# Product 3 of the second sequence matrix made jointly, left forms made as the transform's results come, and results kept on chip

## The chip, the cores and the metric

The kernel runs on one core of one Trainium2 chip, in one launch. The metric is the time of that launch on the device in microseconds (us). Its engines work side by side: TensorE (PE) multiplies matrices, VectorE (DVE) and ScalarE (ACT) do elementwise work, SyncE (SP) and GpSimd (POOL) here only issue transfers (DMA) between the device's memory (HBM) and the chip's. Each engine takes its instructions strictly in the order in which they are written and waits on semaphores for the others.

## What is computed

Two branches of the same shape are mixed by a gate per row. S = 2048 rows, D = 512, F = 1792, all in fp32; A_x is the input of both branches (B_x is not used).

```python
x = A_x
g = _sigmoid((x * gate_w).sum(-1, keepdims=True))
a = einsum("bsd,ed->bse", x, dft_hid_re)           # transform along D
b = einsum("bsd,ed->bse", x, dft_hid_im)
y = einsum("ts,bse->bte", dft_seq_re, a) - einsum("ts,bse->bte", dft_seq_im, b)
gate = x @ W_gate;  up = x @ W_up
h = gate * (gate > 0) * up
out = g * y + (1 - g) * (h @ W_down)
```

The two sequence matrices `dft_seq_re` and `dft_seq_im` (2048x2048, called `cr` and `ci` in the kernel, m = 0 and m = 1) make most of the work.

## The kernel before

**Seven products for eight.** Every large product is cut into 2x2 blocks and made by a scheme of seven block products, numbered 1 to 7 (`ORDER`). It needs sums and differences of the blocks of both factors ahead of the product, and sums of the products behind it. So DVE makes forms of the left factor ("lefts": `l..`, `jl..`), forms of the right factor ("rights": `r..`, `jr..`, `hr..`), and the sums behind the products. For the sequence matrices part of the right forms is made early, during other stages, by `right_sums` (tiles `p..`) and stored to an HBM table `tb`; the table `SUMS` says which and when.

**Three matmuls for one.** To keep fp32's accuracy every operand is split in a high part (rounded to fp32r by ACT, names ending in `h`) and a low part (the rest, by DVE, names ending in `l`); a product is then three matmuls (`PARTS`). A piece of a right factor thus takes a load, an ACT cast and a DVE subtraction of 128x1024 before PE can use it. A matmul here is 128x512 columns wide.

**Stages, in PE's order.** `Direct` and `Block` (bank name `c`) make h for pairs of 128 columns of F, with c the number of the pair and q the half of the rows; h and its forms go to `hd` in HBM. `SpectralBlock` (`a`) makes the transform along D and stores the blocks of its result to `ad`. Two more `Block`s, (1,1) and (0,1), follow as `tail`. `Down` (`z`) multiplies h with W_down and writes (1 - g) times it to `out`. Then come the sequence products: `Sequence` (`z`) makes, for the matrix m and the half p of the output rows, those products among 1 to 7 that are not in `JOINT`; `Joint` (`j..`) makes one output form `of` with all seven products once more on smaller blocks. Before, they run as: Sequence(0,0), Joint of form 3 for m=0, Sequence(0,1), Joint of form 1 for both, Joint of form 2 for m=0, Sequence(1,1), Sequence(1,0), and the last Joint of form 2 for m=1. What m=0 leaves goes to `zd` in HBM and is read back for m=1; results are multiplied by g and added onto `out` by accumulating transfers that POOL issues.

**Who sets the order.** The kernel records its steps with a key (their place, in matmuls) and a planner, `Plan`, puts them in an order before anything runs: it goes through the steps with rough durations of its own (`Step.work`, `Queues`, `LANDING`), sorts DVE and ACT by due times, and gives each tile one of 51 equal pieces of on-chip memory (`UNITS`). Its order alone reaches the chip. SP issues loads, POOL stores and accumulating transfers.

**The start.** Eight matmuls on constant data (`warm`) run while the first pieces of x and of the weights arrive. `Direct` needs the split first blocks `xb11h/l` and `wf0h/l`; the weights of pair c arrive as `wr0`, `wr1` and are split to `w0h`, `w0l` and so on.

Of the kernel before, what the change touches and what calls it, by code (L numbers as in the profile page):

```python
# [9 lines left out]
F32R = mybir.dt.float32r  # L10
# [75 lines left out]
class Step:  # L86


    def __init__(self, key, engine, name, a, k):
# [36 lines left out]
class Queues:  # L126
# [3 lines left out]
    LANDING, LATER = 2.1, 1.5  # L130
# [5 lines left out]
    def serve(self, queues, now, to, done):  # L136
        while True:
            act = [q for q in queues.values() if q and q[0][0] <= now + 1e-9]
            until = min([to, *(q[0][0] for q in queues.values() if q and q[0][0] > now + 1e-9)])
            if act:  # L140
                turn = sum(q[0][2] for q in act)
                n = min(q[0][1] for q in act)
                if now + n * turn <= until:
                    now += n * turn
                    for q in act:
                        q[0][1] -= n
                        if q[0][1] < 1e-9:
                            done(q.pop(0)[3], now)
# [9 lines left out]
    def add(self, step, start):  # L158

        def end(s, t):  # L160
            s.end = t + self.LANDING + (self.LATER if "accum_op" in s.k else 0)

        self.now = self.serve(self.queues, self.now, max(start, self.now), end)
        packets = max(1.0, step.work / (0.166 / 16 * (1.6 if "accum_op" in step.k else 1)))
# [4 lines left out]
class Plan:  # L169
# [4 lines left out]
    MATMUL, WAIT, LANDING = 0.22667, 0.035, 2.1  # L174
# [166 lines left out]
def kernel(ctx: ExitStack, tc, xP, xG, wf, wgu, wd, cr, ci, wri, gw, out):  # L341
# [34 lines left out]
    ad = hbm("ad", 2, 2, 2, 2, P, 4, HD)  # L376
# [3 lines left out]
    lb = hbm("lb", 2, 7, 2, P, 4, HD)  # L380
    tb = hbm("tb", 2, 5, 4, 4, P, 2, N)
    wb = hbm("wb", 7, P, 4, 2, P)
# [90 lines left out]
    class Weights:  # L473
# [24 lines left out]
        def parts(self):  # L498
            return [y for x in self.w for y in x] + [self.w3]
# [24 lines left out]
    JOINT = ((0, 1), (0, 2), (0, 3), (1, 1), (1, 2))  # L524

    SUMS = {(0, 5, 0): 160, (0, 3, 1): 150, (0, 1, 1): 330, (1, 2, 0): 465, (0, 1, 0): 535, (1, 5, 2): 637, (0, 5, 1): 680, (1, 1, 1): 715, (0, 2, 1): 790, (0, 3, 0): 955, (1, 1, 0): 995, (1, 2, 1): 1150, (0, 2, 0): 1270, (1, 5, 1): 1564, (1, 5, 3): 1929, (1, 4, 0): 377}
# [175 lines left out]
    class Spectral:  # L702
# [7 lines left out]

        def prep(self, m, key):
# [11 lines left out]
    class SpectralBlock:  # L723
        def __init__(self, sp, q, ih):
            self.sp, self.q, self.ih = sp, q, ih
            self.s, self.y = buf("s"), buf("y")
            self.o = {b: buf("a" + b, (2, 2, HD)) for b in ("12", "21", "22", "11")}
            self.ps = {k: Pair("a") for k in "ABXDG"}
            for m in ORDER:
# [3 lines left out]
                if m in (2, 7, 3, 4):  # L733
                    op(plan.now + 3, self.out, {2: "11", 3: "12", 4: "21", 7: "22"}[m])
# [729 lines left out]
```

## Time and profile before

| what | us |
|---|---|
| median of 3 runs (lowest, highest) | 785.03 (784.77, 787.34) |
| the profiled execution: own time | 786.9 |
| the profiled execution: span of its instructions | 785.0 |
| PE busy | 777.0 |
| DVE busy | 684.4 |
| ACT busy | 466.1 |
| mean rate of the transfers | 355 GB/s, 278.83 MB in all |

The span runs from the first instruction to the last; times inside it count from its start. The views used here are: the page's totals; the chain of waits, which goes back from the last instruction to what released it, step by step; the timeline of one engine (start, duration, engine, line, operation, output<-inputs, shapes, count, and in brackets the idle time ahead with its releaser); the windows, which give the busy time of every engine in a stretch, the clock that TensorE was granted, and the DMA's share and rate; and the list of waits (who waited for whom: total us, times, longest). All engine code is recorded at one helper line, L123, so instructions are told apart by their tiles. Successive matmuls overlap, so the distance between their starts is their cost, not the duration shown.

### The profile page before, as it was taken

The numbers are of one execution on the slowest core, as the hardware profiler recorded it, in microseconds if no ns is written. First come the engines' busy times: TensorE is split into PE (matmuls) and PEld (weight loads), VectorE is DVE, ScalarE is ACT, GpSimd is POOL, SyncE is SP. The second block draws the span as 40 slices with busy tenths as digits, with TensorE's granted clock in tenths as the row PEclk, the third lists the DMA queues.
The fourth block names the chain that finished last, engine by engine and source line by source line (L and its number), as shares of the span: only waits on it lengthen the run. The fifth ranks groups of instructions, "written<-read, shape, count | busy, mean of one in ns | idle before, by whom it ended". The sixth has DMA issues, their size and how long they took to land.

```text
span 785.0 us, 10154 instructions
## 1 busy us (share of the span) xinstructions
PE 777.0 (99%) x3416; PEld 642.2 (82%) x3416; DVE 684.4 (87%) x773; ACT 466.1 (59%) x653; POOL 122.8 (16%) x197
## 2 busy tenths in 40 slices
PE   9899999999999999999999999999999999999997
PEld 7788888888888888888888888888888887888886
DVE  6899999799699652899996699999989999989896
ACT  5545545343446544566675385487588986855762
POOL 0031332323132222211100000110100000002000
PEclk9999999999999999999999999999999999999999
DMA  8975999999998999989999999999999999999964
GB/s 317 391 308 224 358 401 411 416 390 420 401 360 289 355 405 419 418 328 410 415 298 332 411 395 408 295 299 324 349 374 408 411 410 376 341 359 341 326 207 108
DMA packets 80213, 278.83 MB, mean 355 GB/s; under 512 B 9120, under 2 KB 9888, under 8 KB 80160
## 3 DMA queue, kind: packets, MB, share of 16 engines
q1 hardware_dynamic: 53120, 180.52, 60.0%
q0 software_dynamic: 26896, 97.53, 35.6%
q8 instruction: 27, 0.44, 0.2%
q14 instruction: 26, 0.21, 0.1%
q10 hardware_dynamic: 144, 0.13, 0.0%
HBM read 185.86 MB, written 92.28 MB: 354 GB/s over the span
## 4 chain that ended last, share of the span: by engine, by line
PE 86%; DMA 5%; issue 4%; DVE 3%; ACT 0%; SPq 0%; POOL 0%; DVEq 0%; POOLq 0%; ACTq 0%
PE z L123 35%; PE c L123 31%; PE a L123 10%; PE jB L123 3%; PE jA L123 3%; DMA x<-xP 2%; DMA wr<-wgu 2%; PE jX L123 2%; PE jD L123 1%; DMA out<-z 1%; PE jG L123 1%; DVE r L123 1%; DVE cl L123 1%; DVE jcl L123 1%; SPq L123 0%
## 5 line engine op out<-in xcount | busy, mean ns | idle before, releaser
L123 PE MATMUL z<-ch,ll 128*128 128x512 f32 x484 | 188.4, 389 | 0.3 <-ACT z L123 0.3
L123 PE MATMUL z<-cl,lh 128*128 128x512 f32 x484 | 188.5, 389 | 0.2 <-DVE cl L123 0.2
L123 PE MATMUL z<-ch,lh 128*128 128x512 f32 x484 | 188.3, 389 | 0.0
L123 PEld LDWEIGHTS z<-cl,lh 128*128 128x128 f32 x484 | 90.8, 188 | 19.8 <-DVE cl L123 0.8
L123 PEld LDWEIGHTS z<-ch,ll 128*128 128x128 f32 x484 | 90.8, 188 | 19.5 <-ACT z L123 0.7
L123 PEld LDWEIGHTS z<-ch,lh 128*128 128x128 f32 x484 | 90.8, 188 | 18.8
L123 ACT CAST ch<-r 128x1024 fp32r<-128x1024 f32 x72 | 74.1, 1052 | 40.8 <-DVE r L123 33.6
L123 DVE TENSOR_TENSOR cl<-r,ch 128x1024 fp32r<-128x1024 f32 x72 | 86.9, 1221 | 6.8 <-ACT ch L123 5.1
L123 DVE TENSOR_TENSOR p<-p,p 128x1024 f32<-128x1024 f32 x64 | 77.1, 1220 | 10.6 <-DMA p<-ci 8.6
L123 DVE TENSOR_TENSOR jcl<-jr,jch 128x1024 fp32r<-128x1024 f32 x70 | 83.6, 1219 | 2.0 <-ACT jch L123 1.9
L123 ACT ACTIVATE c<-c 128x512 f32<-128x512 f32 x78 | 45.6, 585 | 63.0 <-PE c L123 50.2
L123 ACT CAST jch<-jr 128x1024 fp32r<-128x1024 f32 x70 | 71.0, 1050 | 4.7 <-DVE jr L123 1.6
L123 DVE TENSOR_TENSOR cl<-hr,ch 128x1024 fp32r<-128x1024 f32 (+1 forms) x56 | 59.6, 1088 | 11.4 <-ACT ch L123 5.3
L123 ACT CAST ch<-hr 128x1024 fp32r<-128x1024 f32 (+1 forms) x56 | 52.0, 945 | 25.5 <-PE z L123 14.1
L123 POOL DMA_DIRECT2D tb<-p x64 | 35.0, 546 | 126.2 <-DVE p L123 115.2
L123 PE MATMUL c<-xh,w2l 128*128 128x512 f32 x104 | 40.8, 393 | 2.5 <-ACT c L123 2.5
L123 PE MATMUL c<-xh,w2h 128*128 128x512 f32 x104 | 40.9, 394 | 0.0
L123 PE MATMUL c<-xl,w2h 128*128 128x512 f32 x104 | 40.9, 394 | 0.0
L123 PE MATMUL c<-xh,w1l 128*128 128x512 f32 x104 | 40.5, 389 | 0.0
L123 PE MATMUL c<-xl,w1h 128*128 128x512 f32 x104 | 40.5, 389 | 0.0
L123 PE MATMUL c<-xh,w1h 128*128 128x512 f32 x104 | 40.5, 389 | 0.0
L123 ACT COPY z<-z 128x512 f32<-128x512 f32 x52 | 29.6, 584 | 15.3 <-PE z L123 14.4
(237 smaller groups left out, 1592.3 us busy)
## 6 DMA issues: line engine op xcount, KB each, us to landing
tb<-p POOLq DMA_DIRECT2D x64, 512.0 KB, 9.6
hr<-hd SPq DMA_DIRECT2D x42, 512.0 KB, 7.4
jr<-tb SPq DMA_DIRECT2D x40, 512.0 KB, 10.2
p<-cr SPq DMA_DIRECT2D x32, 512.0 KB, 8.9
p<-ci SPq DMA_DIRECT2D x32, 512.0 KB, 8.2
hd<-hs POOLq DMA_DIRECT2D x28, 512.0 KB, 8.8
r<-tb SPq DMA_DIRECT2D x24, 512.0 KB, 11.0
l<-ad SPq DMA_DIRECT2D x18, 512.0 KB, 9.1
```

The lines of the kernel that those rows point to most:

```text
L123: getattr(getattr(nc, self.engine), self.name)(*map(ap, self.a), **{k: ap(x) for k, x in self.k.items()})
```

## The change

**Joint stages.** All of forms 1, 2 and 3 are now made jointly for both matrices: `Joint((0,1), of)` three times, and `Sequence` keeps products 5, 6, 7, 4 for m=0 and 7, 6, 5, 4 for m=1. The order is J1, S00, S01, J3, S10, S11 and the last J2. By the program, PE has 3,416 matmuls before and after, but 48 instead of 24 of them are 256 columns wide: that is twelve 512-wide matmuls less.

**Left forms.** `SpectralBlock` now makes the forms 5, 7, 6, 3 of the left factor itself, with 16 more DVE subtractions of 128x1024 behind its blocks, and stores all seven forms to `ad` (28 stores in place of 16); the separate passes that loaded the blocks, made the sums and stored them to `lb` are gone (10 stores and their loads). A sign moves from the evacuation into the weights `v` (`minus`).

**Kept on chip.** What Sequence m=0 leaves stays in its tiles for m=1 (`first`), so 6 stores to `zd`, 4 loads and 2 accumulating transfers go. The weights of c=1 are used three blocks in a row, since block (1,1) moves from the tail to the fourth place, and their 7 stores to `wb` and 7 loads go.

**Planner.** Its durations and the keys (`AT`, `SUMS`) are other numbers, so nearly every order changes. `right_sums` makes 72 forms in place of 64.

In all, DVE has 12 more instructions of 1024 columns and 13 more of 512; SP issues one load of 512 KB and two of 256 KB less, POOL seven transfers of 512 KB less, four of them accumulating ones.

```diff
-            self.work = n * 4 * P / 4096 * 0.166 / 16 * (1.6 if "accum_op" in k else 1)
+            self.work = n * 4 * P / 4096 * 0.160 / 16 * (2 if "accum_op" in k else 1)
...
-            self.work = 0.163 + n * 1.0625e-3
+            self.work = 0.156 + n * 1.039e-3
...
-    LANDING, LATER = 2.1, 1.5
+    LANDING, BUSY = 2.4, 1.8
...
-    MATMUL, WAIT, LANDING = 0.22667, 0.035, 2.1
+    MATMUL, WAIT, LANDING = 0.22667, 0.035, 4.2
...
-    ad = hbm("ad", 2, 2, 2, 2, P, 4, HD)
+    ad = hbm("ad", 2, 7, 2, P, 4, HD)
...
-        def keep(self, key):
-            for n, t in enumerate(self.parts()):
-                op(key + 3 * n, lambda n=n, t=t: store(wb[n], f32(t.all)))
-
-        def fetch(self, key):
-            for k, n in enumerate((0, 1, 4, 5, 2, 3, 6)):
-                op(key + 6 * k, lambda n=n: load(f32(self.parts()[n].all), wb[n]))
...
-    JOINT = ((0, 1), (0, 2), (0, 3), (1, 1), (1, 2))
+    AT = {'gate': (66, 52, 482), 'v': (-90, -80, -52, -36, -20, 6, 10, 38, 44),
...
+        def minus(self, b):
+            im = self.raw[b][:, :, HD:]
+            E().scalar.activation(im, im, AF.Copy, scale=-1.0)
...
-            self.o = {b: buf("a" + b, (2, 2, HD)) for b in ("12", "21", "22", "11")}
+            self.o = {b: buf(f"a{b}", (2, 2, HD)) for b in ("12", "21", "22", "11", 3, 5, 6)}
             self.ps = {k: Pair("a") for k in "ABXDG"}
             for m in ORDER:
                 for i in range(2):
                     pe(6, self.product, m, i)
                     op(plan.now, self.evac, m, i)
-                if m in (2, 7, 3, 4):
-                    op(plan.now + 3, self.out, {2: "11", 3: "12", 4: "21", 7: "22"}[m])
+                if m in (2, 7, 3):
+                    b, to = {2: ("11", 1), 7: ("22", 4), 3: ("12", 2)}[m]
+                    op(plan.now + 3, self.out, b, to)
+            for n, (m, o, a, b) in enumerate(((5, 5, "21", "22"), (7, "21", "21", "11"), (6, 6, "11", 5), (3, 3, "12", 6))):
+                op(plan.now + 6 + 3 * n, lambda o=o, a=a, b=b: combine(self.o[o].all, self.o[a].all, self.o[b].all, -1))
+                op(plan.now + 8 + 3 * n, self.out, o, m)
...
+        def out(self, o, m):
+            store(ad[:, m - 1, self.q, :, 2 * self.ih:2 * self.ih + 2].rearrange("f p t n -> p f t n"), self.o[o].all)
...
+    class Spectrum:
+        def __init__(self, f):
+            self.f, self.t = f, {}
+
+        def fetch(self, m, n, key, step):
+            raw = buf(f"lr{m}", [4, HD])
+            hi, lo = self.t[m, n] = [buf(f"l{x}{m}", [4, HD], F32R) for x in "hl"]
+            op(key, lambda: load(raw.all, ad[self.f, m - 1, n]))
+            op(key + step, lambda: E().scalar.copy(hi.all, raw.all))
+            op(key + step + 5, lambda: E().vector.tensor_sub(lo.all, raw.all, f32(hi.all)))
...
-            self.ORDER = tuple(x for x in ((1, 7, 6, 5, 4, 3) if m else (1, 5, 6, 7, 4)) if (m, x) not in JOINT)
+            self.ORDER = (7, 6, 5, 4) if m else (5, 6, 7, 4)
             self.NEW = () if m else (5, 7)
             if m:
                 self.g = gate_row((2 * p, 2 * p + 1), plan.now + 10)
-                self.z = {b: buf("z") for b in ("11", "22", "12")}
-                for b, key in zip(self.z, (76, 110, 98)):
-                    op(plan.now - key + 48 * (b != "11"), lambda b=b: load(self.z[b].all, zd[self.place(b)]))
+                self.z = {"11": buf("z"), **before.o}
+                op(plan.now - AT["z"][0], lambda: load(self.z["11"].all, zd[self.place("11")]))
...
-            if self.m == 0:
-                op(key, lambda: store(zd[self.place(b)], o.all))
-                return
...
+                op(key, lambda: both(E().vector.tensor_add, o["21"], g, o["21"]))
...
-    sequence = [(1, 0), (2, 0), (2, 1)]
+    sequence = [(1, 0), (2, 0), (2, 1), (1, 1)]
     sequence += [(c, q) for c in range(3, NP) for q in range(2)]
-    tail = [(1, 1), (0, 1)]
-    w = w1
+    tail = [(0, 1)]
+    ws = {1: w1}
...
-            if (c, q) == (1, 0):
-                w.keep(plan.now - 40)
+            Block(q, ws[c])
...
-    Sequence(lefts[0], 0, 0)
-    Joint((0,), 3)
-    for x, key in zip((7, 6, 5, 4, 3), (80, 376, 410, 450, 490)):
-        for k in range(2):
-            lefts[1].fetch(x, k, plan.now + key + 24 * k, 1, 30)
-    Sequence(lefts[0], 0, 1)
-    Joint((0, 1), 1)
-    Joint((0,), 2)
-    Sequence(lefts[1], 1, 1)
-    Sequence(lefts[1], 1, 0)
-    Joint((1,), 2, True)
+    STAGES = ('J1', 'S00', 'S01', 'J3', 'S10', 'S11')
+    first = {}
+    for name in STAGES:
+        if name[:2] == "S0" and not lefts[0].t:
+            for n in range(2):
+                for m, k in zip((5, 6, 7, 4), AT["l0"]):
+                    lefts[0].fetch(m, n, plan.now + k + 14 * n, 30)
+        if name[:2] == "S1" and not lefts[1].t:
+            for n in range(2):
+                for m, k in zip((7, 6, 5, 4), AT["l1"]):
+                    lefts[1].fetch(m, n, plan.now + k + 24 * n, 30)
+        if name[0] == "J":
+            Joint((0, 1), int(name[1]))
+        else:
+            m, p = map(int, name[1:])
+            first[p] = Sequence(lefts[m], m, p, first.get(p))
+    Joint((0, 1), 2, True)
```

Three places where the orders differ. First, SP's queue at the start: `x1..` are the blocks of the second half of x, `wr0` and `wr1` the weights of c=2, `p..` the blocks for `right_sums`. Before:

```order
L123 DMA x112_200<-xP 128x1024 [waits DMAHW1_49]
L123 DMA x121_206<-xP 128x1024 [waits DMAHW2_49]
L123 DMA p12_242<-cr 128x1024 [waits DMAHW3_49]
L123 DMA p22_249<-cr 128x1024 [waits DMAHW4_49]
L123 DMA p11_257<-cr 128x1024 [waits DMAHW5_49]
L123 DMA p12_264<-cr 128x1024 [waits DMAHW6_49]
L123 DMA p22_269<-cr 128x1024 [waits DMAHW7_49]
L123 DMA wr0_277<-wgu 128x1024 [waits DMAHW0_49]
L123 DMA p11_282<-cr 128x1024 [waits DMAHW1_49]
L123 DMA p21_286<-cr 128x1024 [waits DMAHW2_49]
L123 DMA wr1_293<-wgu 128x1024 [waits DMAHW3_49]
```

Now:

```order
L123 DMA x112_196<-xP 128x1024 [waits DMAHW1_49]
L123 DMA x121_204<-xP 128x1024 [waits DMAHW2_49]
L123 DMA wr0_265<-wgu 128x1024 [waits DMAHW3_49]
L123 DMA wr1_276<-wgu 128x1024 [waits DMAHW4_49]
L123 DMA p12_355<-cr 128x1024 [waits DMAHW5_49,DVE_49]
L123 DMA p22_362<-cr 128x1024 [waits DMAHW6_49,PE_49,Activation_49]
L123 DMA p11_369<-cr 128x1024 [waits DMAHW7_49,DVE_49]
L123 DMA p21_396<-cr 128x1024 [waits DMAHW0_49,DVE_49]
L123 DMA p12_469<-ci 128x1024 [waits DMAHW1_49,DVE_49,Activation_49]
L123 DMA p22_475<-ci 128x1024 [waits DMAHW3_49,DMAHW2_49]
```

The weights of c=2 moved from behind five `p` loads, and `wr1` from behind seven, to right behind the x loads; the `p` loads now also wait for memory that DVE, PE or ACT must free. ACT's order around the cast of these weights (`w0h`, between the two copies `c<-c` that PE needs for product 6 of the block with c=1) is the same in both programs:

```order
L123 ACTIVATE c_320<-c_306 128x512 [waits PE_49]
L123 CAST w0h_325<-wr0_265 128x1024 [waits DMAHW3_49]
L123 ACTIVATE c_334<-c_317 128x512 [waits PE_49,Activation_49]
L123 CAST xh1_339<-x111_192 128x1024 [waits DMAHW0_49]
L123 COPY y_350<-c_331 128x512 [waits PE_49]
```

Nothing moved there: the second copy still stands behind the cast.

Second, DVE's first instructions, which split the first blocks for `Direct`. Before:

```order
L123 CAST xb11h_99<-x011_80 128x512 [waits DMAHW0_49]
L123 TENSOR_TENSOR xb11l_105<-x011_80,xb11h_99 128x512 [waits DVE_49]
L123 TENSOR_TENSOR wf0l_113<-wf0_84,wf0h_103 128x512 [waits DMAHW2_49,DMAHW1_49,Activation_49]
L123 CAST xb11h_99<-x011_80 128x512 [waits DMAHW3_49]
L123 TENSOR_TENSOR xb11l_105<-x011_80,xb11h_99 128x512 [waits DVE_49]
L123 TENSOR_TENSOR wf0l_113<-wf0_84,wf0h_103 128x512 [waits DMAHW5_49,DMAHW4_49,Activation_49]
```

Now:

```order
L123 TENSOR_TENSOR wf0l_104<-wf0_82,wf0h_99 128x512 [waits DMAHW2_49,DMAHW1_49,Activation_49]
L123 CAST xb11h_108<-x011_78 128x512 [waits DMAHW0_49]
L123 TENSOR_TENSOR xb11l_113<-x011_78,xb11h_108 128x512 [waits DVE_49]
L123 TENSOR_TENSOR wf0l_104<-wf0_82,wf0h_99 128x512 [waits DMAHW5_49,DMAHW4_49,Activation_49]
L123 CAST xb11h_108<-x011_78 128x512 [waits DMAHW3_49]
L123 TENSOR_TENSOR xb11l_113<-x011_78,xb11h_108 128x512 [waits DVE_49]
```

The low part of the first weights, `wf0l`, which waits for ACT's casts, moved ahead of the cast `xb11h`, without which the first real matmul cannot start.

Third, DVE in the first Sequence stage of m=0 (S00), from the low part `cl5` of the third piece of product 5 on; `r11<-r11,r22` and the like make right forms, `ll..` are the low parts of left forms. Before:

```order
L123 TENSOR_TENSOR cl5_4269<-r11_4140,ch5_4260 128x1024 [waits Activation_49]
L123 TENSOR_TENSOR r11_4167<-r11_4167,r12_4157 128x1024 [waits DMAHW5_49,DMAHW3_49]
L123 TENSOR_TENSOR r12_4046<-r12_4046,r22_4064 128x1024
L123 TENSOR_TENSOR cl5_4295<-r11_4167,ch5_4286 128x1024 [waits PE_49,Activation_49]
L123 TENSOR_TENSOR z22_4178<-z22_4178,gg_3857 128x1024
L123 TENSOR_TENSOR cl7_4312<-r12_4046,ch7_4297 128x1024 [waits PE_49,Activation_49]
L123 TENSOR_TENSOR r12_4089<-r12_4089,r22_4103 128x1024 [waits DMAHW6_49,DMASW2_49]
L123 TENSOR_TENSOR r11_4083<-r11_4083,r22_4064 128x1024
L123 TENSOR_TENSOR cl7_4337<-r12_4089,ch7_4328 128x1024 [waits DMASW5_49,Activation_49]
L123 TENSOR_TENSOR r11_4109<-r11_4109,r22_4103 128x1024
L123 TENSOR_TENSOR cl6_4356<-r11_4083,ch6_4341 128x1024 [waits PE_49,Activation_49]
L123 TENSOR_TENSOR z21_4197<-z21_4197,gg_3857 128x1024
```

Now:

```order
L123 TENSOR_TENSOR cl5_4667<-r11_4531,ch5_4658 128x1024 [waits Activation_49]
L123 TENSOR_TENSOR r11_4558<-r11_4558,r12_4543 128x1024 [waits DMAHW6_49,DMAHW4_49]
L123 TENSOR_TENSOR r12_4449<-r12_4449,r22_4465 128x1024 [waits DMAHW2_49]
L123 TENSOR_TENSOR cl5_4692<-r11_4558,ch5_4684 128x1024 [waits Activation_49]
L123 TENSOR_TENSOR ll6_4701<-lr6_4563,lh6_4690 128x1024 [waits DMAHW7_49,Activation_49]
L123 TENSOR_TENSOR cl7_4710<-r12_4449,ch7_4698 128x1024 [waits PE_49,Activation_49]
L123 TENSOR_TENSOR r12_4487<-r12_4487,r22_4496 128x1024
L123 TENSOR_TENSOR ll6_4727<-lr6_4573,lh6_4706 128x1024 [waits DMAHW0_49,PE_49,Activation_49]
L123 TENSOR_TENSOR r11_4481<-r11_4481,r22_4465 128x1024
L123 TENSOR_TENSOR cl7_4753<-r12_4487,ch7_4730 128x1024 [waits Activation_49]
L123 TENSOR_TENSOR r11_4508<-r11_4508,r22_4496 128x1024
L123 TENSOR_TENSOR cl6_4774<-r11_4481,ch6_4755 128x1024 [waits Activation_49]
```

Two multiplications by g (`z..<-z..,gg`) of the stage ahead left this place, and low parts of left forms, each with a load of its own to wait for, came in.

More of the change, by code (lines that the diff above doesn't have):

```diff
@@ L147, in serve @@
                         if q[0][1] < 1e-9:
-                            done(q.pop(0)[3], now)
+                            s = q.pop(0)[3]
+                            done(s, now, any(x and x[0][0] <= now for x in queues.values()))
                     continue
@@ L158, in add, with end @@
     def add(self, step, start):
-        def end(s, t):
-            s.end = t + self.LANDING + (self.LATER if "accum_op" in s.k else 0)
+        def end(s, t, busy):
+            s.end = t + self.LANDING + (self.BUSY if busy else 0)
         self.now = self.serve(self.queues, self.now, max(start, self.now), end)
-        packets = max(1.0, step.work / (0.166 / 16 * (1.6 if "accum_op" in step.k else 1)))
+        packets = max(1.0, step.work / (0.160 / 16 * (2 if "accum_op" in step.k else 1)))
         self.queues.setdefault(step.engine, []).append([start, packets, step.work / packets, step])
@@ L1092, in __init__ @@
         def __init__(self, ms, of, last=False):
-            self.ms, self.of, self.last, self.base, self.lead = ms, of, last, plan.now, 130 if last else 60
+            self.ms, self.of, self.last, self.base, self.keys = ms, of, last, plan.now, AT[f"J{of}"]
             self.ORDER = (1, 7, 6, 5, 2, 3, 4) if last else (1, 5, 6, 2, 7, 3, 4)
```

121 lines of the change are left out of this document (34 added, 87 removed).

## The prediction

> **What bounds the kernel now.** I read the page's totals first, then the chain of waits, then the engines' timelines at each place where the chain leaves PE. From the page:
>
> ```profile
> span 785.0 us, 10154 instructions
> PE 777.0 (99%) x3416; PEld 642.2 (82%) x3416; DVE 684.4 (87%) x773; ACT 466.1 (59%) x653; POOL 122.8 (16%) x197
> DMA packets 80213, 278.83 MB, mean 355 GB/s; under 512 B 9120, under 2 KB 9888, under 8 KB 80160
> ```
>
> TensorE is busy nearly always; VectorE is next at 87%. From the chain of waits (start us, us, what):
>
> ```profile
> 20.05 14.96 DMA wr<-wgu
> ...
> 35.03 0.02 ACT w0h L123
> ...
> 35.98 0.59 ACT c L123
> ...
> 36.62 204.53 PE c L123 x894
> 241.15 76.16 PE a L123 x336
> ...
> 355.39 176.80 PE z L123 x780
> ```
>
> From 36.62 us on the chain is matmul behind matmul, 176.80 / 780 = 0.2267 us each. Ahead of that it runs through a load of weights that landed at 35.0 us, their cast on ACT, and a copy of a PSUM bank that stood behind the cast. So the time is the number of matmuls times 0.2267 us, plus the places where PE stands. The largest is this one, on PE's and ACT's timelines:
>
> ```profile
> 33.50 0.39 PE L123 MATMUL c<-xl,w2h 128*128 128x512 f32 x1
> 33.73 0.39 PE L123 MATMUL c<-xh,w2h 128*128 128x512 f32 x1
> 36.62 0.53 PE L123 MATMUL c<-xh,w2l 128*128 128x512 f32 x1 [2.50 <-ACT c L123]
> ...
> 37.80 0.63 PE L123 MATMUL c<-xh,w2l 128*128 128x512 f32 x1
> 38.23 0.63 PE L123 MATMUL c<-xl,w2h 128*128 128x512 f32 x1
> ...
> 40.36 0.40 PE L123 MATMUL c<-xb21h,w0l 128*128 128x512 f32 x1
> ```
>
> ```profile
> 30.44 0.58 ACT L123 ACTIVATE c<-c 128x512 f32<-128x512 f32 x1
> 35.03 1.04 ACT L123 CAST w0h<-wr 128x1024 fp32r<-128x1024 f32 x1 [4.01 <-DMA wr<-wgu]
> 35.98 0.58 ACT L123 ACTIVATE c<-c 128x512 f32<-128x512 f32 x1
> ```
>
> PE stood from 33.96 to 36.62, and then ran at half pace (0.43 us from start to start) until 40.36. From 33.73 to 40.36 there are ten steps: 6.63 us instead of 10 x 0.2267 = 2.27, so the gap costs 4.36 us in all. The second place is the end of the kernel, by the windows of the sequence stages (busy us by engine and count, clock, DMA share, GB/s):
>
> ```profile
> 595.00:633.00 38.00, 38.00 (x169) 31.45 (x169) 38.00 (x44) 35.54 (x46) 0.53 (x1) 1.00 1.03 409
> ...
> 652.00:706.00 54.00, 53.68 (x237) 43.92 (x236) 49.33 (x47) 37.27 (x47) 5.13 (x6) 1.00 1.04 354
> 706.00:761.00 55.00, 54.82 (x242) 45.10 (x241) 50.82 (x51) 37.34 (x47) 6.78 (x8) 1.00 0.99 316
> ```
>
> In the last two PE is idle for 0.32 + 0.18 = 0.5 us. The first shows that DVE can work 38 us without a pause while PE loses nothing.
>
> **The change part by part.**
>
> *Matmuls.* Twelve fewer: 12 x 0.2267 = -2.72 us, all on the path.
>
> *The weights of c=2.* They stand in SP's queue where the first `p` load stood. SP's timeline says when that place came and when its load had landed:
>
> ```profile
> 14.26 4.83 SPq L123 DMA_DIRECT2D p<-cr  x5
> 20.05 0.33 SPq L123 DMA_DIRECT2D wr<-wgu  x1
> ...
> 25.73 0.33 SPq L123 DMA_DIRECT2D wr<-wgu  x1
> 27.61 0.33 SPq L123 DMA_DIRECT2D p<-cr  x1
> ```
>
> The place was issued at 14.26. The load issued at 25.73 waits for DMAHW3, the semaphore of exactly that place, so a load issued there had landed by 25.7; the one behind it, where `wr1` now stands, by 27.6 (DMAHW4). ACT comes to the cast at 31.0 (30.44 + 0.58), so it finds its data, and the gap goes: -4.36 us. The seven `wb` stores that ran beside these loads are gone too. The `p` loads, now behind, feed `right_sums`, whose results are read hundreds of us later; their new waits for memory hold up, on SP, only each other and the weights of c=3, which the blocks (2,1) and (1,1) now give one block more (19 us) of time. What ends last at 34 us is then the ordinary copy of the PSUM bank.
>
> *The start.* DVE now makes `wf0l` ahead of `xb11h`. DVE's and PE's timelines:
>
> ```profile
> 3.44 0.43 DVE L123 CAST xb11h<-x 128x512 fp32r<-128x512 f32 x1 [2.44 <-DMA x<-xP]
> ...
> 4.76 0.69 DVE L123 TENSOR_TENSOR wf0l<-wf,wf0h 128x512 fp32r<-128x512 f32 x1 [0.16 <-ACT wf0h L123]
> 5.37 0.42 DVE L123 CAST xb11h<-x 128x512 fp32r<-128x512 f32 x1
> ```
>
> ```profile
> 1.06 3.78 PE L123 MATMUL warm<-warm 128*128 128x512 f32 x8 [1.06 <-DVE warm L123]
> 4.63 1.82 PE L123 MATMUL c<-xb11h,wf0h 128*128 128x512 f32 x4
> 6.29 1.08 PE L123 MATMUL c<-xb11l,wf0h 128*128 128x512 f32 x4
> ```
>
> `wf0l` cannot start before 4.76 (ACT's cast), the cast `xb11h` follows at 5.37 and ends at 5.79, so the first real matmul starts at about 5.85, not 4.63: +1.22 us. All that follows is queued behind it on PE. In the trace the first four real matmuls run at half pace (1.66 us for four) up to 6.29. If the full pace comes at the same moment, the later start skips most of that half pace, which saves up to 4 x 0.2 = 0.8: +0.4. If the pause of a microsecond puts full pace off by as long as it took after 36.62 (3.74 us, nine steps that are each 0.2 slow), it costs 1.8 less the 0.8 already paid: +2.2. I take +1.22, between the two.
>
> [...]
>
> *Left forms.* 16 more DVE subtractions in the transform. Two windows of that stage:
>
> ```profile
> 280.00:300.00 20.00, 20.00 (x90) 16.57 (x89) 7.71 (x10) 8.43 (x16) 4.23 (x7) 1.00 1.03 405
> 300.00:320.00 20.00, 20.00 (x90) 16.57 (x89) 7.28 (x8) 9.09 (x16) 6.11 (x10) 1.00 1.03 418
> ```
>
> DVE has 25 us free in these 40, against 16 x 1.14 = 18: hidden, 0 us. Without that cover the forms would be late, but their first reader (Joint 1) comes over 100 us later. POOL's 12 more `ad` stores are outweighed by the 10 `lb` and 7 `wb` stores that leave; transfers as a whole fall by 9 x 0.5 = 5 MB of 278.83. No transfer is on the path between 36.62 and the last stages, so I give that nothing, nor the `zd` traffic that goes; both only make landings earlier.
>
> *The sequence stages.* Here DVE has more to do in less time. Its steps, from start to start:
>
> ```profile
> 23.56 0.68 DVE L123 TENSOR_TENSOR h<-dg,c 128x512 f32<-128x512 f32 x1
> 24.16 1.22 DVE L123 TENSOR_TENSOR x<-x,x 128x1024 f32<-128x1024 f32 x1
> 25.30 1.22 DVE L123 TENSOR_TENSOR xl<-xs,xh 128x1024 fp32r<-128x1024 f32 x1
> ```
>
> 0.60 us for 512 columns and 1.14 for 1024. From J1 up to the start of J2, DVE now has 179 of 1024 and 71 of 512: 246 us of work beside 250.3 us of matmuls, 98%. Before, from S00 to the last Joint, it was 190 and 67: 256 us beside 272, 94%. The tightest stage is S00, where the order shows it: from `cl5_4667` to the last `cl7` of that product come 23 steps of 1.14 = 26.2 us, and PE needs 108 matmuls = 24.5 us between the two that read them; before, at the same place, 22 steps for the same 24.5 us. With no lead that is 1.7 us of waiting. At the very end the last low part `jcl4` stands twelve steps (10.4 us) behind the one that PE reads 3.3 us earlier, for which I add 0.7. So PE waits about 2.4 us instead of the 0.5 of before: +1.9. Bounds: 0 us of waiting (-0.5), as in the window 595:633; and DVE's idle time of before coming back on top of the work. From the waits of DVE between 460 and 765 us (total, times, longest), first and last of nine rows:
>
> ```profile
> DVE cl L123 <- ACT ch L123: 5.1, 7, 1.5
> ...
> DVE jt L123 <- ACT jt L123: 0.2, 1, 0.2
> ```
>
> The nine come to 13.2 us. In the same span of matmuls (307 us) DVE's work is now 302, so 13.2 - 5 = 8 us of waiting (+7.5). I take +1.9, since the nearer row is the one in which DVE was full and PE lost nothing.
>
> *Sum.* -2.72 - 4.36 + 1.22 + 1.9 = -4.0 us on the span of 785.0, so 781.0. The profiled execution's own time is 786.9 us, 1.9 above its span and the median of the runs (785.03); I take the difference off the median: 781.0.
>
> **The rivals.**
>
> *DVE bounds the end.* The eight us above, and with DVE at 98% one of PE's pauses reaching the length of the one at 33.96, which adds 4.36 - 2.66 = 1.7 of half pace: -2.72 - 4.36 + 1.22 + 7.5 + 1.7 = +3.3, 788.4 us, slower. It decides from 8.2 us of further waiting on. For it: 98%, and two new chains of load, cast, subtraction in S00. Against: 38 us at 100% without loss.
>
> *The early gap stays*, because another load or cast takes the weights' place in front of the copy: 781.0 + 4.36 = 785.4, no change. For it: ACT's order there is unchanged, the copy still stands behind the cast. Against: five us between landing and use.
>
> *The clock at the start*: 781.0 + 1.0 = 782.0.
>
> *Nothing waits at the end* and the start costs 0.4: -2.72 - 4.36 + 0.4 - 0.5 = -7.2, 777.8.
>
> **How the numbers follow.** Forecast 0.55 (779 to 784), the clock 0.11, no waiting 0.12, the early gap 0.10, DVE 0.12. A measurement can tell about 0.3%, 2.4 us. Below 782.7 lie the clock, no waiting and most of the forecast: faster 0.74. The early gap and the forecast's upper end: same 0.14. Slower: 0.12. The range, 777.5 to 786.5, holds all but the DVE case and a little at either end.
>
> **What would show it.** Right: no PE gap and no half pace between 30 and 45 us, with `w0h` following the first copy at once; the first real matmul near 5.8 us; PE idle of two or three us in all, in S00 and at the end, with DVE `cl` as releaser; PE still the chain. Wrong: ACT idle on `wr` near 31 us; DVE idle on loads in the sequence stages, with PE waiting over 8 us there; or half pace again in any later stage.

## The result, and the profile after

The kernel after takes 781.78 us in the median of six runs (780.1 to 782.43); the kernel before, run beside it, 785.7 us (784.45 to 788.04). The ratio is 0.9942, with a 95% interval of 0.9922 to 0.9963: faster by 0.6%, some 4 us. The profiled execution took 782.31 us, its span is 780.5 us, 4.5 us shorter than before.

The page's totals of the kernel after:

```profile
span 780.5 us, 10195 instructions
PE 774.1 (99%) x3416; PEld 640.3 (82%) x3416; DVE 706.8 (91%) x798; ACT 467.4 (60%) x649; POOL 119.6 (15%) x190
DMA packets 78774, 274.12 MB, mean 351 GB/s; under 512 B 8960, under 2 KB 9728, under 8 KB 78720
```

DVE went from 87% to 91%, and PE still has no room. The chain of waits of the kernel after (start us, us, what) shows where the path leaves PE:

```profile
1.19 2.77 DMA wf<-wf
3.98 0.77 ACT wf0h L123 x2
5.95 252.59 PE c L123 x1104
...
760.08 1.22 DVE jr L123
...
771.84 1.15 DVE jcl L123
773.03 3.75 PE jH L123 x29
```

The load of weights, ACT's cast and the copy that stood in this chain before 36.62 us are gone: PE is on it without a break from its first real matmul, at 5.95 us, to 759 us. New in it is a stretch that is nearly all DVE, from there to the last matmuls.

**The early gap.** ACT's timeline and the window from 30 to 45 us (busy us by engine and count: PE, PEld, DVE, ACT, POOL; then clock, DMA share, GB/s) of the kernel after, with the same window of the kernel before behind it:

```profile
31.46 0.58 ACT L123 ACTIVATE c<-c 128x512 f32<-128x512 f32 x1 [1.26 <-PE c L123]
31.95 1.04 ACT L123 CAST w0h<-wr 128x1024 fp32r<-128x1024 f32 x1
32.89 0.59 ACT L123 ACTIVATE c<-c 128x512 f32<-128x512 f32 x1
```

```profile
30.00:45.00 15.00, 15.00 (x68) 12.43 (x67) 13.45 (x17) 11.34 (x18) 0.00 (x0) 1.00 0.21 73
```

```profile
30.00:45.00 15.00, 12.50 (x49) 9.83 (x48) 11.54 (x14) 8.59 (x14) 3.17 (x6) 0.89 0.89 357
```

The cast `w0h` follows the copy ahead of it at once, and PE is busy for all of the 15 us. Before, it was idle for 2.5 of them, and the clock granted to it was 0.89 of the full one on average.

**The start.** PE's timeline of the kernel after:

```profile
1.06 3.78 PE L123 MATMUL warm<-warm 128*128 128x512 f32 x8 [1.06 <-DVE warm L123]
5.95 2.05 PE L123 MATMUL c<-xb11h,wf0h 128*128 128x512 f32 x4 [1.11 <-DVE xb11h L123]
7.79 1.91 PE L123 MATMUL c<-xb11l,wf0h 128*128 128x512 f32 x4
9.50 1.52 PE L123 MATMUL c<-xb11h,wf0l 128*128 128x512 f32 x4
10.86 1.07 PE L123 MATMUL c<-xb11h,wf0h 128*128 128x512 f32 x4
```

PE pauses 1.1 us behind the warm-up. Four matmuls then take 1.84 us (5.95 to 7.79), the half pace, and the full pace (0.91 us for four) comes only near 10.4 us. The 13th real matmul starts at 10.86; before, at 8.11. So this start costs 2.75 us in this execution: 1.32 because the first real matmul is later, 1.43 because half pace lasts longer.

**The sequence stages.** Windows of the kernel after, columns as above:

```profile
488.00:526.00 38.00, 38.00 (x169) 31.49 (x168) 37.96 (x40) 28.47 (x37) 1.06 (x2) 1.00 1.00 388
526.00:570.00 44.00, 44.00 (x194) 35.91 (x193) 43.30 (x39) 26.89 (x31) 5.08 (x7) 1.00 1.02 359
...
738.00:776.00 38.00, 37.55 (x186) 31.81 (x185) 36.22 (x37) 21.98 (x26) 0.85 (x1) 1.00 0.63 224
```

And the longest of PE's waits (who waited for whom: us in total, times, longest):

```profile
PE c L123 <- DVE xb11h L123: 1.1, 1, 1.1
...
PE jH L123 <- DVE jcl L123: 0.5, 1, 0.5
```

DVE is full in J1 and S00 (37.96 of 38, 43.30 of 44), yet the only wait that the list names in a late stage is the half microsecond at the very end:

```profile
772.18 0.40 PE L123 MATMUL jH<-jch,jt 128*128 128x256 f32 x2
773.03 0.39 PE L123 MATMUL jH<-jcl,jt 128*128 128x256 f32 x1 [0.45 <-DVE jcl L123]
773.26 0.40 PE L123 MATMUL jH<-jch,jt 128*128 128x256 f32 x2
```

These matmuls of 256 columns start 0.12 us apart elsewhere in this product. Here three of them take 1.08 us (772.18 to 773.26) instead of 0.36, so the wait costs 0.7 us and not only its idle 0.45. Besides, PE loses 0.3 us in S00 by the distances between starts, 1.0 in all; before, it lost 1.1 us in its late stages.

The two profiled executions so differ by 2.75 (start) - 4.36 (early gap) + 1.0 - 1.1 (late waits) = -1.7 us. PE's last matmul starts at 776.48 instead of 780.81, so 2.6 us are left for the twelve matmuls less, and 0.26 us come from a shorter tail of the last stores: -4.6 in all. The 2.6 fit the spacing: 24 matmuls that start 0.12 instead of 0.2267 us apart save 2.56.

### The profile page after: what moved, and what is told of

It reads as the page before. It is cut to its first block, busy times and chain, and to the rows that moved or that the text cites. A ratio compares the mean times of both kernels' runs of the same rounds, so it can differ in the third digit from the quotient of the medians.

```text
span 780.5 us, 10195 instructions
## 1 busy us (share of the span) xinstructions
PE 774.1 (99%) x3416; PEld 640.3 (82%) x3416; DVE 706.8 (91%) x798; ACT 467.4 (60%) x649; POOL 119.6 (15%) x190
## 4 chain that ended last, share of the span: by engine, by line
PE 97%; DVE 2%; DMA 0%; issue 0%; ACT 0%; SPq 0%; ACTq 0%
PE z L123 39%; PE c L123 35%; PE a L123 10%; PE jB L123 3%; PE jA L123 3%; PE jX L123 2%; PE jD L123 2%; PE jG L123 1%; DVE jcl L123 1%; DVE jo L123 0%; PE jH L123 0%; DMA wf<-wf 0%; DVE jr L123 0%; ACT wf0h L123 0%; DVE wf0l L123 0%
## 5 line engine op out<-in xcount | busy, mean ns | idle before, releaser
L123 PE MATMUL z<-cl,lh 128*128 128x512 f32 x452 | 176.1, 390 | 0.0
L123 PE MATMUL z<-ch,lh 128*128 128x512 f32 x452 | 175.9, 389 | 0.0
L123 PE MATMUL z<-ch,ll 128*128 128x512 f32 x452 | 175.8, 389 | 0.0
L123 DVE TENSOR_TENSOR jcl<-jr,jch 128x1024 fp32r<-128x1024 f32 x84 | 99.5, 1216 | 0.9 <-issue 0.3
L123 PEld LDWEIGHTS z<-cl,lh 128*128 128x128 f32 x452 | 84.8, 188 | 17.9 <-DVE cl L123 0.6
L123 ACT CAST jch<-jr 128x1024 fp32r<-128x1024 f32 x84 | 85.4, 1053 | 16.8 <-PE z L123 5.8
L123 DVE TENSOR_TENSOR p<-p,p 128x1024 f32<-128x1024 f32 x72 | 86.8, 1219 | 5.6 <-DMA p<-ci 4.9
L123 ACT CAST ch<-r 128x1024 fp32r<-128x1024 f32 x64 | 65.9, 1051 | 36.7 <-DVE r L123 26.3
L123 DVE TENSOR_TENSOR cl<-r,ch 128x1024 fp32r<-128x1024 f32 x64 | 76.9, 1219 | 0.6 <-ACT ch L123 0.4
L123 ACT COPY a<-a 128x512 f32<-128x512 f32 x40 | 23.1, 579 | 25.9 <-PE a L123 21.0
```

The lines of the kernel that those rows point to most:

```text
L123: getattr(getattr(nc, self.engine), self.name)(*map(ap, self.a), **{k: ap(x) for k, x in self.k.items()})
```

## Experiments

In the kernels that follow, single steps are moved in the order that `Plan` has made, right behind `self.order()` in `Plan.run`, and nothing is planned anew. `find(engine, tile, n)` gives the n-th step of an engine that writes a tile, `ahead` and `behind` put a step beside another one. Times are compared by their ratio to the kernel before, run on the same chip at the same time; where times are differences of ratios, they are taken of 786 us.

### The loads of c=2's weights alone

```diff
+ p = next(s for s in self.steps if s.engine == "sync" and s.writes[0].base.name.startswith("p"))
+ for n in range(2):
+     self.ahead(self.find("sync", f"wr{n}", 1), p)
```

> The kernel before, with the two loads of c=2's weights ahead of SP's first p load, and nothing else moved. Theory (the early gap was the place of these loads in SP's queue): w0h's cast finds its data, PE has no pause and no half pace between 30 and 45 us, and the time falls by 4.36 us: ratio 0.9944. Rival (DMA load: the gap went because transfers as a whole fell and the stores of c=1's weights are gone): with these stores still there the loads land late all the same or another load is late instead, ACT waits for DMA near 31 us, and the time falls by less than 2 us.

Measured: 782.0 us beside 786.03, ratio 0.995 (0.9935 to 0.9965), 4.0 us less. ACT's timeline and the window of this kernel:

```profile
30.16 0.58 ACT L123 ACTIVATE c<-c 128x512 f32<-128x512 f32 x1
30.67 1.03 ACT L123 CAST w0h<-wr 128x1024 fp32r<-128x1024 f32 x1
31.61 0.57 ACT L123 ACTIVATE c<-c 128x512 f32<-128x512 f32 x1
```

```profile
30.00:45.00 15.00, 15.00 (x68) 12.43 (x67) 14.96 (x19) 8.97 (x15) 3.70 (x7) 1.00 1.03 416
```

The gap is gone although the DMA engines are full there (share 1.03, with the stores of c=1's weights still running). It was the place of two loads in SP's queue, not the amount of transfers. These two moved loads give nearly as much as the whole change.

The kernel before does not lose 4.36 us in every execution. Each run comes with the mean clock that TensorE was granted. Of the 17 runs of the kernel before that stand beside this one, ten have a clock of 0.996 to 0.998 and take 785.7 to 787.89 us (median 786.46); seven have 0.999 or 1.0 and take 784.15 to 784.9 (median 784.43). The profiled execution is of the first kind (0.997), and in it the clock is below 0.99 only between 30 and 50 us, around the gap. (The half pace at the start does not show in this figure: it is 1.00 there.) If the pause is the same in both kinds, it cost some 2.7 us in either, and the half pace behind it another 1.7 us in the first kind only. The medians fit: the two moved loads gain 4.5 us beside the first kind and 2.4 beside the second. That the other runs of the first kind lost their clock at this same place is inferred from the one trace. Their share differs between the sets of runs (here 10 of 17, later 17 of 23 and 5 of 9), and the ratios carry it with them.

### DVE's order at the start, in both kernels

In the kernel after, `wf0l` back behind `xb11l`:

```diff
+ for n in range(2):
+     self.behind(self.find("vector", "wf0l", n), self.find("vector", "xb11l", n))
```

> The kernel after, with DVE's wf0l behind xb11l, as in the kernel before. Theory: no pause between warm-up and real matmuls, full pace from about 6.3 us, the 13th real matmul at about 8.1 us, and the time falls by 2.75 us against the kernel after, to about 779.0 us: ratio to the kernel before 0.991. Rival (the order of the start matters only by the 1.22 us): 780.6 us, ratio 0.993. Second rival (a gain at the start is lost in the late stages, where DVE is full: PE comes sooner, DVE does not): 781 to 782 us, with PE idle in the stage S00 by 2 us more than in the kernel after.

Measured: 780.25 us, ratio 0.9924 (0.9908 to 0.994). The same kernel was run once more:

> The kernel after with the start of before, once more, to stand beside the next kernel on the same chip. Theory: ratio to the kernel before 0.992 as in its first run, between 0.9908 and 0.994; the 13th real matmul between 7.6 and 9.4 us, since the end of the half pace varies from run to run, and one wait of 0.5 us at the end of PE's work. Rival (the first run was lucky): ratio as the kernel after, 0.9942.

Measured: 779.26 us, ratio 0.9919 (0.9904 to 0.9934). Against 0.9942 for the kernel after, the order of the start costs 0.0018 to 0.0023, or 1.4 to 1.8 us: between the 1.22 of the prediction and the 2.75 of the one trace. PE's timeline of the first of the two runs:

```profile
1.06 3.78 PE L123 MATMUL warm<-warm 128*128 128x512 f32 x8 [1.06 <-DVE warm L123]
4.64 1.96 PE L123 MATMUL c<-xb11h,wf0h 128*128 128x512 f32 x4
6.41 1.17 PE L123 MATMUL c<-xb11l,wf0h 128*128 128x512 f32 x4
...
8.33 1.08 PE L123 MATMUL c<-xb11h,wf0h 128*128 128x512 f32 x4
```

PE has no pause, and full pace comes near 6.4 us. In neither run does PE wait in S00, so nothing of the gain is lost there: the second rival falls.

The other way round, the kernel before with the start of the kernel after:

```diff
+ for n in range(2):
+     w, x = self.find("vector", "wf0l", n), self.find("vector", "xb11h", n)
+     i, j = self.steps.index(x), self.steps.index(w)
+     late = [s for s in self.steps[i:j] if s.engine in ("vector", "tensor")]
+     rest = [s for s in self.steps[i:j] if s.engine not in ("vector", "tensor")]
+     self.steps[i:j + 1] = rest + [w] + late
```

> The kernel before, with DVE's wf0l ahead of xb11h, as in the kernel after, and nothing else moved. Theory (the later start also puts off full pace): the pause between the warm-up matmuls and the first real one keeps the half pace until about 10.3 us, the 13th real matmul starts at about 10.9 us instead of 8.1, and the time grows by 2.75 us: ratio 1.0035. Rival (the prediction's term: full pace comes at the same moment or shortly after): 1.22 us, ratio 1.0016, 13th real matmul at about 9.3 us.

Measured: 784.88 us beside 786.03, ratio 0.9987 (0.9975 to 0.9998). Both expectations missed: the time does not grow, it falls a little. PE's and ACT's timelines of this kernel:

```profile
5.96 1.17 PE L123 MATMUL c<-xb11h,wf0h 128*128 128x512 f32 x4 [1.17 <-DVE xb11h L123]
...
8.80 1.07 PE L123 MATMUL c<-xb11h,wf0h 128*128 128x512 f32 x4
...
34.41 0.39 PE L123 MATMUL c<-xh,w2h 128*128 128x512 f32 x1
36.37 0.50 PE L123 MATMUL c<-xh,w2l 128*128 128x512 f32 x1 [1.56 <-ACT c L123]
36.70 0.39 PE L123 MATMUL c<-xl,w2h 128*128 128x512 f32 x1
```

```profile
34.79 1.04 ACT L123 CAST w0h<-wr 128x1024 fp32r<-128x1024 f32 x1 [4.33 <-DMA wr<-wgu]
```

The weights land when they did before (the cast starts at 34.79 us against 35.03). PE comes 0.69 us later to the place where it waits for them (13th matmul 8.80 against 8.11), so it waits less, and behind this shorter pause it is not at half pace: from 36.70 on a step takes 0.23 us, where after the longer pause eight steps took 0.43 and one 0.33. From 34.41 to 36.70 there are two steps in 2.29 us: the gap costs 1.84 instead of 4.36. All twelve runs of this kernel have a granted clock of 0.999 or 1.0. Beside the runs of the kernel before with such a clock (784.43) it is 0.45 us slower, beside the others (786.46) 1.6 us faster: by these clocks the time falls because no run goes to half pace at the gap here. The two terms do not add: the 0.69 us that PE loses ahead of this wait, it gets back at the wait. A second thing is seen here: PE paused 1.17 us behind its warm-up, and yet the full pace came with the second matmul.

### Both on the kernel before

> The kernel before, with the loads of c=2's weights ahead of SP's first p load and DVE's wf0l ahead of xb11h. Theory (the terms add up): -4.36 + 2.75 = -1.6 us against the kernel before, 784.1 us by its median of 785.7; and what is then left to the kernel after, 2.3 to 3 us, is the 12 matmuls (2.72) and the late stages (0.3). Rival (the rest of the change costs time, which these two hide): as the kernel after, or faster, 781.8 us or less.

Measured: 782.78 us beside 786.31, ratio 0.9957 (0.9942 to 0.9972). By the ratio the time falls by 3.4 us, not by 1.6, and what is left to the kernel after (0.9942) is 1.2 us, with intervals that hold both 0 and 3. The trace is clearer. In the profiled execution the first real matmul starts at 6.57, the 13th at 10.73 and the last at 779.01; in the kernel after the 13th starts at 10.86 and the last at 776.48. Between the two the kernel after is 2.66 us shorter: 0.1 are late waits (1.1 against 1.0), and 2.55 are left for the twelve matmuls. So the theory holds for executions with a late full pace; but the six runs fall in two groups, two at 784.84 (the profiled one among them) and four at 782.63 to 782.86, which fits a cheaper start in most of them. The kernel after has four runs at 781.65 to 782.43 (the profiled one among them) and two at 780.1 and 780.35. Group beside group it is 2.7 and 2.4 us faster, as the trace says; the ratio gives less because the groups are mixed otherwise. The groups were made after the runs were seen, and only the later kind is in a profile.

### More warm-up matmuls

```diff
-    WARM = 8
+    WARM = 11
```

> The kernel after with 11 warm-up matmuls instead of 8: they fill the pause of 1.1 us ahead of the first real matmul, which still waits for DVE. Theory (the pause puts off the full pace): the pace is full from about 6.3 us on, the 13th real matmul starts at about 8.9 us instead of 10.9, and the time falls by 2.0 us against the kernel after, to about 779.8 us. Rival (the pace is half for a fixed time after the first matmul, or the pause has nothing to do with it): half pace until about 10.3 us as before, time as the kernel after, 781.8 us.

Measured: 780.87 us, ratio 0.9936 (0.992 to 0.9952), 0.5 to 0.9 us less than the kernel after. PE's timeline:

```profile
1.06 5.06 PE L123 MATMUL warm<-warm 128*128 128x512 f32 x11 [1.06 <-DVE warm L123]
6.04 1.66 PE L123 MATMUL c<-xb11h,wf0h 128*128 128x512 f32 x4
...
9.36 1.07 PE L123 MATMUL c<-xb11h,wf0h 128*128 128x512 f32 x4
```

With the pause filled, the first real matmul is no earlier (6.04), but the full pace comes at 7.0 us instead of 10.4 and the 13th matmul starts at 9.36 instead of 10.86. The direction is the theory's; the size, 1.5 in the trace, is less than the 2.0 expected. The intervals of the two ratios overlap, so the runs alone do not show the gain.

The profiles together show where single executions differ (the pause that PE's timeline lists ahead of the first real matmul, the moment at which the full pace begins, to some 0.2 us, and the start of the 13th real matmul, all in us):

| kernel | pause | full pace from | 13th matmul |
|---|---|---|---|
| before | none | 6.3 | 8.11 |
| before, loads moved | none | 5.1 | 7.65 |
| after, start of before (twice) | none | 6.4, 5.9 | 8.33, 8.06 |
| after, start of before, end moved | none | 4.1 | 7.28 |
| after, 11 warm-up matmuls | none | 7.0 | 9.36 |
| before, start of after | 1.2 | 6.1 | 8.80 |
| before, both | 1.7 | 9.5 | 10.73 |
| after | 1.1 | 10.4 | 10.86 |
| after, DVE work in S00, J1, S11 | 1.1 to 1.2 | 10.0, 9.3, 10.2 | 10.68, 10.33, 10.76 |

Without a pause, full pace comes between 4.1 and 7.0 us, with a pause between 9.3 and 10.4, and once at 6.1. The moment varies: six starts without a pause spread over 2.9 us. Where a pause fell in, full pace came about 4 us later in five of six (9.9 us on average against 5.8). What sets the moment in a single execution, no trace here shows.

### More work for DVE at three places

The edit for S00; for J1 the place is `("jcl6", 0)`, for S11 `("cl5", 20)`.

```diff
+ k = self.steps.index(self.find("vector", "cl5", 10))
+ g = next(b for b in self.bufs if b.name == "gwt").all
+ for n in range(4):
+     self.steps.insert(k, Step(0, "vector", "tensor_add", (g, g, g), {}))
```

> The kernel after with four more additions of 128x512 on DVE (2.4 us at 0.60 from start to start), in place on a row of weights that has no later reader, right ahead of the third cl5 of the stage S00. Theory (DVE's lead is just used up in S00: PE waited there for cl7 with 0.06 us between the end on DVE and the start on PE): PE's idle time in S00 grows by 2.3 us and the time by as much, 784.1 us against 781.8. Rival A (DVE has room everywhere, the small waits in S00 are ordinary latency): under 0.5 us. Rival B (DVE bounds all later stages, one pause begets others): over 4 us.

> The kernel after with the same four additions (2.4 us), right ahead of the first jcl6 of the stage J1, near 489 us, where DVE's results lie about 9 us ahead of PE. Theory (DVE works without a pause from there to S00, so that its lead of J1 is what S00 lives on): PE waits nowhere in J1, but 2.3 us more in S00, 784.1 us. Rival (the lead of J1 is room to spare, each stage stands by itself): 0, 781.8 us.

> The kernel after with the same four additions (2.4 us), right ahead of the first cl5 of the stage S11, near 700 us, where DVE's results lie 7 to 11 us ahead of PE. Theory (DVE is off the path there, and has some 2.9 us without work from 695 us to the end): 0 to 0.6 us more, 781.8 to 782.4. Rival B (DVE bounds all later stages): 2.4 us more, 784.2.

Measured: in S00 784.59 us, ratio 0.9978 (0.9966 to 0.999), 2.8 us more than the kernel after by the ratios; in J1 784.81 us, ratio 0.9975 (0.9964 to 0.9986), 2.6 us more; in S11 783.22 us, ratio 0.9953 (0.9937 to 0.9969), 0.9 us more. PE's timelines, the rows with a wait; first with the work in S00, then with the work in J1:

```profile
534.24 0.50 PE L123 MATMUL z<-cl,lh 128*128 128x512 f32 x1 [0.46 <-DVE cl L123]
541.05 0.50 PE L123 MATMUL z<-cl,lh 128*128 128x512 f32 x1 [1.06 <-DVE cl L123]
```

```profile
530.40 0.50 PE L123 MATMUL z<-cl,lh 128*128 128x512 f32 x1 [0.16 <-DVE cl L123]
533.88 0.50 PE L123 MATMUL z<-cl,lh 128*128 128x512 f32 x1 [0.47 <-DVE cl L123]
540.70 0.50 PE L123 MATMUL z<-cl,lh 128*128 128x512 f32 x1 [1.04 <-DVE cl L123]
```

They are the same waits at the same places. In both kernels PE loses 2.6 us in S00 by the distances between starts, where it lost 0.3 without the work: 2.3 us more. The work added for J1 ran on DVE from about 480 us on, some 50 us ahead of these waits; it is paid in S00 to the same amount, and PE waits nowhere in J1. So DVE does reach S00 with a lead; it is the lead of J1, and DVE works on it without a pause. How long it is, and where it ends, is seen in the kernel after, on DVE's and PE's timelines of the third `cl5` and the second `cl7`:

```profile
526.92 1.23 DVE L123 TENSOR_TENSOR cl<-r,ch 128x1024 fp32r<-128x1024 f32 x1
...
537.57 1.22 DVE L123 TENSOR_TENSOR cl<-r,ch 128x1024 fp32r<-128x1024 f32 x1
```

```profile
530.61 0.39 PE L123 MATMUL z<-cl,lh 128*128 128x512 f32 x1
...
538.85 0.50 PE L123 MATMUL z<-cl,lh 128*128 128x512 f32 x1
```

The third `cl5` is ready at 528.15, and PE reads it at 530.61: a lead of 2.5 us. From there DVE needs nine steps (10.65 us) to the second `cl7`, PE 36 matmuls (8.2 us). The lead is gone exactly there: `cl7` ends at 538.79, PE reads it at 538.85. In the kernels with more work the waits at 540.70 and 541.05 are those for this same piece, and behind it DVE gains on PE again. The rival that each stage stands by itself falls, and so does the one that more work begets more pauses.

In S11 the same work costs less than half. The rows of this kernel:

```profile
539.66 0.50 PE L123 MATMUL z<-cl,lh 128*128 128x512 f32 x1 [0.82 <-DVE cl L123]
...
774.85 0.39 PE L123 MATMUL jH<-jcl,jt 128*128 128x256 f32 x1 [1.47 <-DVE jcl L123]
```

```profile
738.00:776.00 38.00, 36.53 (x175) 30.64 (x174) 37.84 (x40) 22.48 (x26) 0.84 (x1) 1.00 0.63 216
```

The wait at the end grows from 0.45 to 1.47 us of idle time (from 0.7 to 1.7 by the distances between starts), since DVE now is full there (37.84 of 38, before 36.22). I had expected at most 0.6: the free time before the last stage was counted with the free time behind the last `jcl`, which helps nobody. The wait of 0.82 us in S00 lies far ahead of the edit, in the same order of DVE as in the kernel after. It moves with DVE's own waits between 520 and 530 us: here DVE stood 1.00 us in all for a cast of ACT (`lh`) and two loads of `r`, and PE lost 1.2 us in S00; in the kernel after DVE stood 0.26 us for a load of `r`, and PE lost 0.3; in the three profiles with the earlier start DVE did not stand, and PE lost nothing, with 11 warm-up matmuls 0.1. Why these loads and this cast come later in one execution than in another stays open.

### The last low part ahead of the last sums

```diff
+ last = self.find("vector", "jcl4", -1)
...
+ for s in reversed(back):
+     self.behind(s, last)
```

`back` are the four steps of `jo0` and `jo1` that stand right ahead of `last`.

> The kernel after with the start of before, and with the last jcl4 on DVE moved ahead of four steps of jo0 and jo1 (2.6 us), which only the last stores read. Theory: PE's wait of 0.5 us for that jcl4 goes, the stores keep their place, and the time falls by 0.5 us against the kernel beside it. Rival (the stores of jo then land last): the end of PE's work comes 0.5 us sooner, the time stays.

Measured: 778.55 us (777.88 to 778.66) beside 779.26 for the kernel with the start alone, ratio to the kernel before 0.9902 (0.9886 to 0.9918). No wait of PE behind 600 us is left in the list, and PE's last matmul starts at 772.57 instead of 773.30. SP issues four of the last stores of `jo` from 770.39 us on (770.42 in the kernel beside it), and ACT the very last one at 773.34 instead of 774.08. The rival falls: the span ends with the work, at 776.7 instead of 778.1 us. The gain of 0.7 us is what this wait cost by the distances between starts; the 0.5 expected was its idle time alone. The intervals of the two ratios overlap. This is the fastest kernel of the study. Its start shows once more how a wait for a fixed moment takes back a gain:

```profile
1.05 3.48 PE L123 MATMUL warm<-warm 128*128 128x512 f32 x8 [1.05 <-DVE warm L123]
4.43 1.20 PE L123 MATMUL c<-xb11h,wf0h 128*128 128x512 f32 x4
...
7.28 1.07 PE L123 MATMUL c<-xb11h,wf0h 128*128 128x512 f32 x4
...
10.64 1.20 PE L123 MATMUL c<-xb21h,wf1h 128*128 128x512 f32 x4 [0.48 <-ACT wf1h L123]
```

Here full pace came at about 4.1 us, during the warm-up matmuls, and the 13th matmul 0.78 us earlier than in the run beside it. But PE then waits for `wf1h`, whose first matmul starts at 10.64 us against 10.78, and the distances between starts lose 0.75 us there.

## Why the prediction was right, and where it was not

**The total.** 781.0 was forecast, 781.78 measured, with the sign, and with the mechanism that was held to be the largest. But two of its terms were wrong in opposite directions in the profiled execution, and they hid each other there: the start by +1.5 and the sequence stages by -2.0. That 781.0 came so near is in part luck.

**The weights of c=2 (-4.36): right in mechanism, and in size for part of the runs.** The gap cost 4.36 in the trace of before and nothing after. Alone, the two moved loads gave 4.0 us, 4.5 beside the runs of the kernel before with a lowered clock and 2.4 beside the others. The sum took the term from an execution with half pace behind the gap (786.9 us) and subtracted it from a median of 785.03, which by its time belongs to the runs without. The reading that carried it was SP's timeline: the semaphore of the place in the queue showed when a load issued there would have landed.

**Matmuls (-2.72): right, a little large.** 2.6 us are left for them in the trace. The narrow matmuls behind the last joint product start 0.12 us apart, not 0.113, which for 24 more of them is 0.16 us. No run has this term alone.

**The start (+1.22): too small in the trace, nearly right in the runs.** The trace shows +2.75, above the upper bound of 2.2; the ratios of the runs give 1.4 to 1.8. The step that failed is the bound: "If the pause of a microsecond puts full pace off by as long as it took after 36.62". That one duration was taken for a constant. With the pause, full pace came anywhere from 6.1 to 10.4 us in six profiles. The term itself was a choice between two bounds and holds no mechanism of its own; that the runs lie near it is luck. The rival of 782.0 us took the upper bound, which by the 8.11 of before puts the 13th matmul at 10.3 us: five of the six have it between 10.33 and 10.86, one at 8.80. No trace here shows what sets the one apart.

**The sequence stages (+1.9): wrong in size, -0.1 instead.** The step that failed is "With no lead that is 1.7 us of waiting". S00 is indeed where DVE's reserve ends, but DVE brought a lead of 2.5 us from J1, and PE lost 0.3 us. The 23 steps for 108 matmuls also span too much: the tight stretch is its beginning, nine steps for 36 matmuls, where DVE falls 2.1 us behind by the same count (9 x 1.14 - 36 x 0.2267) and 2.5 in the trace, with a wait of 0.26 us for a load; the rest brings some of it back. The end (0.7) was right with 0.7. And what PE lost before was not 0.5 but 1.1 us: windows of busy time don't show a matmul that starts late and is slow behind a wait, the distances between starts do. The row that was quoted, 38 us of full DVE without loss to PE, said that a lead can exist; the sum should have asked how long it was, not whether.

**Left forms and transfers (0): right.** The transform's windows (280 to 300 and 300 to 320 us) show PE busy for all of its 20 us in the kernel after too, with 15.2 and 14.4 us of DVE beside it. The first experiment shows a full DMA at the early gap without harm. No run has this part of the change alone.

**What no step said:** that the terms at 5 us and at 34 us are not independent. In the kernel before, the later start cost nothing (ratio 0.9987), since the wait for the weights took it in, and behind the shorter pause (1.73 us) the pace was still full.

## What to carry to other kernels

Before a loss early in a kernel is added to the sum, look for the next wait for something that comes at a fixed time, such as a load: up to there losses and gains can be swallowed, as the 0.69 us of the later start were here (ratio 0.9987 with the wait in place), and they count when that wait is gone (0.0018 to 0.0023 of the time). For an engine at 98% of its time, ask how far its results lie ahead of the reader where the dense stretch begins, count its steps against the reader's from there piece by piece, and put in a known amount of extra work at two places: if both are paid at the same later place, that place is the bound and the stretch between lives on one lead. And where a change of nearly the whole order gains half a per cent, first try the two or three single steps that the chain of waits names: two moved loads gave nearly as much here as the whole.

## What was not expected of the hardware

- With a pause of 1.1 to 1.7 us behind eight warm-up matmuls, TensorE came to full pace at 9.3 to 10.4 us in five of six profiles and at 6.1 in one; without it the full pace came between 4.1 and 7.0.
- At full pace a pause of 1.73 us (34.64 to 36.37) left the pace at 0.23 us a step; behind one of 2.66 us (33.96 to 36.62) it was half for 3.7 us. By the granted clock of the runs half pace followed the first in none of twelve (0.999 or 1.0), the second in ten of 17 (0.996 to 0.998). The sum had counted it in every run.
- The runs of one kernel fall in groups 2 us apart (after: 780.1 and 780.35, then 781.65 to 782.43), which fits the spread of the full pace's beginning; but that beginning is seen only in profiled executions, and no profile of the kernel after fell in the lower group.
